# Exp units on GpSimd outside the span of branch B, a scaling step moved to GpSimd, and corrected operation times in a planned kernel

## Chip, cores, metric

One core of a Trainium2 chip. The metric is device time in microseconds (us) of the whole program. TensorE's clock is granted by a throttle; each run comes with the mean granted share (1.0 is full speed).

## The reference, cut to what matters

Two attention branches over the same input x (2048 tokens, width 512, 32 heads of 16), mixed by a gate:

```python
g = sigmoid((x * gate_w).sum(-1, keepdims=True))
a = A(x)   # full softmax attention: 32 heads x 2048 x 2048 scores
b = B(x)   # each token sees 8 earlier tokens (offsets 0, 2, .. 14)
return g * a + (1 - g) * b
```

Branch A needs 32 x 2048 x 2048 exponentials. The kernel cuts them into 2048 units of 128 keys x 512 queries. Branch B has 16 tiles of 128 tokens; it is mostly elementwise work.

## The kernel before

All instructions are recorded by a planner that runs while the kernel is built. Jobs (Python generators) yield requests such as `("dve", priority, duration, function)`. The planner keeps a clock for each engine, picks the next job from the durations written in the source, and so fixes the instruction order on every engine. A duration in the source is therefore no work, but it decides the order.

The exps of branch A take two ways. ScalarE takes three units or two in one instruction (buffers `ring` -> `pT`):

```python
def act_tail(k, parts, rname, rslot, ring, n):
    ...
    def f():
        st["pT"] = work.tile([128, 3 if k % 2 == 0 else 2, QW], BF16, name="pT", tag=pname, bufs=2)
        A.activation(out=st["pT"][:, 0:n, :], in_=ring[:, 0:n, :], func=ACT.Exp,
                     scale=LN2 / 128.0, bias=-VOFF * LN2 / 128.0)
    yield ("act", k, 0.050 + 0.4267 * n, f)
    ...
```

VectorE takes single units ("riders" that TensorE adds to a ring step when a `w` bank of PSUM is free), as a cubic polynomial on the bits, in four operations that read PSUM:

```python
def dve_unit(p, t, j, s, ds, wt, n):
    lo = wt[:].bitcast(U16).rearrange("p (n two) -> p n two", two=2)[:, :, 0]
    ...
    yield ("dve", pr, VP, e1)                  # ta = lo * A3
    yield ("dve", pr, VP, lambda: e23(A2))     # ta = (ta + A2) * lo
    yield ("dve", pr, VP, lambda: e23(A1))     # ta = (ta + A1) * lo
    yield ("dve", pr, VP, e4)                  # pd = ta + const + scores, as 16-bit integers
```

Branch B runs on GpSimd, but its softmax has one wide step on VectorE, which the plan takes for 0.34 us:

```python
def b_attn(t, rel, prio):
    ...
    def attn():
        V.scalar_tensor_tensor(out=lg[:], in0=lg[:], scalar=omg[:, t:t + 1], in1=bc(st["ss"]), op0=ALU.mult,
                               op1=ALU.mult)
    yield ("dve", prio, 0.34, attn)
    ...
```

The planner also issues "fillers" into planned gaps of TensorE: matmuls with a zero weight tile (`acc<-ident,z`) that add nothing and are meant to keep the clock up.

## Time and profile before

| | before |
|---|---|
| first three runs | 877.56, 877.6, 881.56 us |
| the profiled run | 881.81 us (span 880.0), granted clock 0.98 |
| exp units: ScalarE / VectorE | 1814 in 726 instructions / 234 |
| first exp starts, last exp ends | 19.1, 868.3 us |

The profiled run is one of the slower ones of this kernel.

The page's span and busy times: engine, busy us, share of the span, instructions.

```profile
span 880.0 us, 15956 instructions
PE 771.3 (88%) x6062; PEld 268.1 (30%) x6062; DVE 767.9 (87%) x1346; ACT 842.6 (96%) x758; POOL 619.4 (70%) x594
```

The page's slices of before: each digit is a fortieth of the span, busy share in tenths; PEclk is the granted clock.

```profile
POOL 2000283899797889898898989897989898965000
PEclk9799999999999999999999999879999999999999
```

ScalarE (ACT) has almost no room. GpSimd (POOL) is idle in the second to fourth slices and in the last three. The clock is below full in a few slices.

The page's chain of waits, by engine and then by engine, tile and line:

```profile
ACT 48%; PE 22%; issue 19%; DVE 11%; DMA 0%; ACTq 0%
ACT pT L288 47%; PE w L288 8%; PE ring L288 7%; PE acc L288 6%; DVE ta L288 5%; DVE pd L288 1%; DVE lg L288 1%; PE heat L288 1%; PE last L288 0%; ACT lg L288 0%; DVE accS L288 0%; DVE ssum L288 0%; PE xt L288 0%; DVE kvs L288 0%; DVE kpk L288 0%
```

Half of the chain is the exps.

Groups of instructions of before with forms kept apart: engine, operation, out<-in, shapes, count, then busy us and the mean ns of one, then idle time before them and what ended it.

```profile
L288 ACT ACTIVATE pT<-ring 128x1536 bf16<-128x1536 f32 x363 | 544.9, 1501 | 13.8 <-PE ring L288 7.4 <-PE w L288 3.2 <-PE acc L288 0.3
L288 ACT ACTIVATE pT<-ring 128x1024 bf16<-128x1024 f32 x362 | 390.5, 1079 | 6.1 <-PE ring L288 3.5 <-PE w L288 1.9
...
L288 DVE SCALAR_TENSOR_TENSOR lg<-lg,omg,ssum 128x256 f32<-128x256 f32 x16 | 14.2, 886 | 0.1
```

The exps overlap their neighbours, so the durations overstate their cost. From start to start the median is 1.33 us for three units and 0.90 us for two, 2.23 us a pair. The scaling took 0.89 us on average; single ones took 0.465 to 1.531 us.

Busy times of before in stretches (PE, PEld, DVE, ACT, POOL, then granted clock, DMA share, GB/s):

```profile
30.00:35.00 5.00, 5.00 (x36) 1.37 (x35) 2.22 (x6) 4.52 (x5) 0.00 (x0) 0.50 0.00 0
...
285.00:290.00 5.00, 4.40 (x25) 1.03 (x25) 3.12 (x5) 3.22 (x4) 4.69 (x6) 0.66 0.15 39
580.00:585.00 5.00, 4.80 (x31) 1.22 (x28) 3.84 (x7) 4.19 (x5) 4.92 (x6) 0.50 0.00 0
```

In these stretches TensorE had half its clock for all or part of the time, and ScalarE was idle for 0.5 to 1.8 of 5 us. In the trace's clock record of this run there are five such stretches before the tail, 3.4, 6.8 or 10.2 us long, and only the values 1.0 and 0.5. That agrees with the Trainium skill's "TensorE: Matmul & The Clock Gate" (Part 1), which has a free-running window of 3413 ns and two clock states.

### The profile page before, as it was taken

To read this page: it belongs to the slowest core of one execution; us is meant where nothing else is said; L and a number is where in the kernel's file an instruction comes from. 1 tells how busy PE (TensorE), PEld (TensorE's weight loads), DVE (VectorE), ACT (ScalarE), POOL (GpSimd) and SP (SyncE) were. 2 spreads that over 40 slices of the span, in tenths; PEclk is the share of its full clock that TensorE was granted. 3 is DMA by queue.
4 is the path that set the end of the run, shared out by engine and by line. 5 is a ranking of instruction groups with operands and counts; after the bars stand their busy time and mean duration, and the time that the engine had idled before them with its cause. 6 is when DMAs were issued, how large, how long until landed. Compare 5 with 4: busy or idle time off the path is not lost.

```text
span 880.0 us, 15956 instructions
## 1 busy us (share of the span) xinstructions
PE 771.3 (88%) x6062; PEld 268.1 (30%) x6062; DVE 767.9 (87%) x1346; ACT 842.6 (96%) x758; POOL 619.4 (70%) x594
## 2 busy tenths in 40 slices
PE   8999889998898888889899998888798988888886
PEld 4232333333223232223333232223232222223222
DVE  4789899988989799989987888988988989989885
ACT  5999999999999999999999999999999999999995
POOL 2000283899797889898898989897989898965000
PEclk9799999999999999999999999879999999999999
DMA  8002203331414230321131312303021230200000
GB/s 288 2 1 96 80 24 120 108 122 29 150 32 144 67 115 19 114 67 42 30 104 31 125 50 95 103 7 109 1 74 60 84 115 7 64 4 7 1 1 25
DMA packets 55710, 59.78 MB, mean 68 GB/s; under 512 B 3649, under 2 KB 52289, under 8 KB 55633
## 3 DMA queue, kind: packets, MB, share of 16 engines
q1 hardware_dynamic: 54816, 58.50, 21.0%
q8 instruction: 47, 0.77, 0.4%
q10 hardware_dynamic: 816, 0.26, 0.1%
q14 instruction: 31, 0.25, 0.1%
HBM read 46.14 MB, written 12.62 MB: 67 GB/s over the span
## 4 chain that ended last, share of the span: by engine, by line
ACT 48%; PE 22%; issue 19%; DVE 11%; DMA 0%; ACTq 0%
ACT pT L288 47%; PE w L288 8%; PE ring L288 7%; PE acc L288 6%; DVE ta L288 5%; DVE pd L288 1%; DVE lg L288 1%; PE heat L288 1%; PE last L288 0%; ACT lg L288 0%; DVE accS L288 0%; DVE ssum L288 0%; PE xt L288 0%; DVE kvs L288 0%; DVE kpk L288 0%
## 5 line engine op out<-in xcount | busy, mean ns | idle before, releaser
L288 ACT ACTIVATE pT<-ring 128x1536 bf16<-128x1536 f32 x726 | 830.1, 1290 | 19.9 <-PE ring L288 10.9
L288 PE MATMUL ring<-qt,kt_all 32*128 32x512 bf16 x1878 | 294.2, 387 | 87.0 <-ACT pT L288 77.0
L288 DVE SCALAR_TENSOR_TENSOR ta<-ta,w 128x512 f32<-128x512 f32 x468 | 308.3, 679 | 5.0
L288 POOL TENSOR_TENSOR prod<-prod 128x512 f32<-128x512 f32 (+1 forms) x208 | 241.7, 1175 | 6.3
L288 PE MATMUL acc<-pT,vp_all 128*17 128x512 bf16 x1814 | 230.8, 390 | 0.1
L288 PEld LDWEIGHTS <-kt_all 32*128 32x128 bf16 x2112 | 104.8, 91 | 334.7 <-issue 320.0
L288 DVE TENSOR_SCALAR ta<-w 128x512 f32<-128x512 uint16 x234 | 157.9, 684 | 39.8 <-PE w L288 38.6
L288 PE MATMUL acc<-ident,z 128*32 128x512 bf16 (+6 forms) x750 | 168.6, 340 | 5.9 <-DVE accS L288 5.4
L288 DVE SCALAR_TENSOR_TENSOR pd<-ta,w 128x512 uint16<-128x512 f32 x234 | 156.4, 678 | 2.6
L288 POOL TENSOR_TENSOR prod<-ksh,qb 128x512 f32<-128x512 bf16 x128 | 145.7, 1164 | 11.4 <-DVE ta L288 9.3
L288 POOL TENSOR_TENSOR prod<-vsh,lg 128x512 f32<-128x512 bf16 x128 | 136.7, 1100 | 10.5 <-DVE lg L288 8.2
L288 PE MATMUL w<-qt,kt_all 32*128 32x512 bf16 x234 | 88.0, 389 | 1.0 <-DVE osb L288 0.6
L288 POOL TENSOR_SCALAR mq<-qpk 128x512 f32<-128x512 bf16 x12 | 7.4, 615 | 108.0 <-DVE qpk L288 108.0
L288 PE MATMUL acc<-pd,vp_all 128*17 128x512 bf16 x234 | 81.1, 390 | 0.2
L288 PEld LDWEIGHTS <-z 128*32 128x32 bf16 x774 | 51.9, 95 | 82.7 <-issue 65.5
L288 PEld LDWEIGHTS <-vp_all 128*17 128x17 bf16 x2048 | 44.5, 88 | 90.3 <-issue 88.0
L288 PE MATMUL w<-bw,xT 128*128 128x512 bf16 x192 | 51.2, 390 | 3.2 <-DVE pd L288 1.6
L288 PEld LDWEIGHTS <-xT 128*128 128x128 bf16 x512 | 31.7, 98 | 38.1 <-issue 25.1
L288 POOL TENSOR_TENSOR lg<-lg,mx 128x256 f32<-128x256 f32 x16 | 10.1, 630 | 37.4 <-DVE mx L288 37.3
L288 DVE CAST kvs<-w 128x512 bf16<-128x512 f32 x32 | 21.9, 686 | 12.5 <-PE w L288 12.5
L288 DVE COPY accS<-acc 128x512 f32<-128x512 f32 (+1 forms) x32 | 21.5, 673 | 1.8 <-ACT accS L288 1.5
L288 POOL TENSOR_TENSOR obb<-ob,prod 128x512 bf16<-128x512 f32 x16 | 20.4, 1272 | 1.3
(110 smaller groups left out, 437.4 us busy)
## 6 DMA issues: line engine op xcount, KB each, us to landing
ksh<-kv_scr SPq DMA_DIRECT2D x16, 1024.0 KB
vsh<-kv_scr SPq DMA_DIRECT2D x16, 1024.0 KB
kv_scr<-kvs SPq DMA_DIRECT2D x16, 256.0 KB
kt_all<-k_scr SPq DMA_DIRECT2D x6, 512.0 KB
q_scr<-qpk SPq DMA_DIRECT2D x24, 128.0 KB
qt<-q_scr SPq DMA_DIRECT2D x24, 128.0 KB
xr<-in_A_x_dram SPq DMA_DIRECT2D x4, 512.0 KB
out_dram<-osb SPq DMA_DIRECT2D x14, 128.0 KB
```

What stands on the lines that cost most here:

```text
L288: return chain_on(self._key, f(*a, **k))
```

## The change

The intent: GpSimd is idle before branch B starts and after it ends, so let it compute exp units there. VectorE copies the scores from PSUM to SBUF (a buffer that branch B uses for its values, lent outside its span), and GpSimd evaluates the cubic in six operations. Branch B's scaling moves from VectorE to GpSimd as two operations. GpSimd's durations in the plan are set to what traces show, and what GpSimd delivers is used 2.5 us later than planned (slack). A rule adds a filler to a ring step when the plan sees TensorE busy under 40% of the last 3.4 us.

```diff
-    LAT = {"pe": 0.17, "act": 0.22, "dve": 0.12, "pool": 0.12, "sp": 0.08}
+    LAT = {"pe": 0.17, "act": 0.22, "dve": 0.12, "pool": 0.02, "sp": 0.08}
...
+                if (shut is not None and any(row_left[shut])
+                        and P.have(P.now + dur) < THIN * P.HAM):
+                    more += fill_pass(0.2134, P.now) + 0.01
...
+    def pool_unit(p, t, j, s, hs, wt, n):
+        sc, y, z = psc[0][:, hs, :], psc[0][:, 2, :], psc[0][:, 3, :]
+        ...
+        yield ("dve", 39, VP, lambda: V.tensor_copy(out=sc, in_=wt[:]))
+        yield ("rel", "w", s)
+        ...
+        yield ("pool", 0, 0.70, lambda: G.tensor_scalar(out=y, in0=lo, scalar1=YA, scalar2=YA * YS, op0=ALU.mult,
+                                                        op1=ALU.add))
+        yield ("pool", 0, 1.34, lambda: G.tensor_tensor(out=z, in0=y, in1=y, op=ALU.mult))
+        yield ("pool", 0, 0.70, lambda: G.tensor_scalar(out=z, in0=z, scalar1=1.0, scalar2=YB, ...))
+        yield ("pool", 0, 1.34, lambda: G.tensor_tensor(out=z, in0=z, in1=y, op=ALU.mult))
+        yield ("pool", 0, 1.34, lambda: G.tensor_tensor(out=z, in0=z, in1=sc, op=ALU.add))
+        ...                                        # fin: pd = z + const, as 16-bit integers, 0.70
+        yield ("delay", SLACK)
...
-                yield ("pool", gp, 1.11, mul_k(hf, w_))
-            yield ("pool", gp, 1.22, add_k(8, 0, 2))
+                yield ("pool", gp, 1.12, mul_k(hf, w_))
+            yield ("pool", gp, 1.30, add_k(8, 0, 2))
... (the other durations of GpSimd likewise)
-        def attn():
-            V.scalar_tensor_tensor(out=lg[:], in0=lg[:], scalar=omg[:, t:t + 1], in1=bc(st["ss"]), ...)
-        yield ("dve", prio, 0.34, attn)
+        yield ("pool", -4, 0.40, lambda: G.tensor_scalar(out=st["ss"][:], in0=st["ss"][:], scalar1=omg[:, t:t + 1], ...))
+        yield ("pool", -4, 0.72, lambda: G.tensor_tensor(out=lg[:], in0=lg[:], in1=bc(st["ss"]), op=ALU.mult))
...
         yield ("rel", "ob", 0)
+        yield ("delay", SLACK)
```

## The prediction

> **What bounds it now.** ScalarE. The page's busy table has it busy 842.6 of 880.0 us; the chain of waits runs through its exps (pT) for 47% of the span. They start at 19.12 us and end at 868.3 us, with 11.7 us of tail: 726 instructions, 1814 of the 2048 units of 128x512; VectorE does 234. In an undisturbed stretch of the timeline (834.76 on, 30 instructions in 33.58 us) one averages 1.12 us, a unit 0.45 us. 726 x 1.12 = 813 us; the other 36 us are branch B's 16 small exps (0.47 us each), about 14 us of visible waits, and late starts that the pipeline partly hides. The windows tie the worst waits to TensorE's granted clock: 0.50 to 0.66 around 25-37, 285 and 580-590 us. In the waits view nobody waits notably for GpSimd; it waits 37 us for VectorE's row maximum. It is idle before 88 us (but for setup) and after 804 us.
>
> **What changes.** Counted in the built programs' instruction order, 22 units go to GpSimd, 12 before branch B and 10 after. But VectorE's fall from 234 to 224, so ScalarE loses only 12 units, five instructions (726 to 721).
> - A GpSimd unit, from like operations: three two-input (1.28 us each) and three one-input (0.62 to 0.72): about 5.9 us. The Trainium skill's GPSIMD Engine Reference (Specifications) gives GpSimd no PSUM access, hence a VectorE copy, 0.68 us; a VectorE unit costs 4 x 0.68 = 2.7 us. 22 units fill 130 us of idle GpSimd.
> - Branch B's attention scaling leaves VectorE (16 x 0.89 us) for two GpSimd operations (estimate 0.4 + 0.65 us). The same section says that GpSimd contends with VectorE operations with two SBUF inputs; the trace agrees: this one took 0.465 to 1.531 us.
> - VectorE: -27 us of exps, +15 of copies, -14 of scaling: about 742 busy. GpSimd: +147, about 766.
> - GpSimd's corrected times only reorder. GpSimd was never late for anyone, so they remove no wait directly. The slack protects TensorE's in-order queue. Filler matmuls are added where TensorE has been thinly busy, but filler columns barely change (204k to 199k).
>
> **On the critical path.** Five exp instructions at 1.12 us, less 0.5 us for the odd single-unit one that goes: about 5 us. I add 2 us for waits, from a looser VectorE and better placed filler. Start and tail are unchanged; VectorE's relief is off the path.
>
> **Prediction.** 877.6 - 7 = 870.5 us, range 864 to 877. Faster by over 2% (under 860): 0.08; within 2%: 0.90; slower: 0.02.
>
> **What the profile would show.** Right: 721 pT instructions, the last ending near 861 to 862 us, pT busy about 824 us; the three-plus-two pair still 2.24 us; GpSimd working from near 25 to near 855 us; tail 11 to 12 us; no wait for a GpSimd result over 1 us. Wrong on waits: clock dips (windows under 0.7) gone or new, 1 to 3 us of exp time each. Wrong on unit cost: GpSimd operations over 1.4 us, with TensorE or VectorE waiting for them.
>
> **What would make it wrong.** Clock dips falling elsewhere: before's three runs already spread 4 us (877.56 to 881.56). If those at 25-37 and 580-590 us vanish, it ends near 864. If GpSimd in branch B, with about 1 us more per tile and nearly full (36 to 38 of each 40 us), falls behind, the in-order VectorE waits for its logits and all slips, to 877 or more.

## The result, and the profile after

| | before | after |
|---|---|---|
| first rounds, median (range) | 878.73 (877.56 to 881.56), 4 runs | 867.38 (865.5 to 869.42), 4 runs |
| ratio | | 0.9867, 95% interval 0.9832 to 0.9901 |
| later rounds | 879.91 (876.83 to 882.41), 11 runs | 870.11 (868.11 to 872.68), 6 runs |
| ratio | | 0.9891, 95% interval 0.9869 to 0.9914 |

A ratio is the mean time of one kernel's runs over that of the other's of the same rounds, so it is not quite the ratio of the medians. The gain is 1.1 to 1.3%, 10 to 11 us; both medians lie in the predicted range of 864 to 877 us.

The page's span and busy times of after:

```profile
span 865.4 us, 16034 instructions
PE 755.1 (87%) x5977; PEld 268.1 (31%) x6038; DVE 751.1 (87%) x1312; ACT 836.0 (97%) x753; POOL 750.4 (87%) x758
```

The slices of after, for GpSimd and the clock:

```profile
POOL 2586995999898989999999999998999999978883
PEclk9999999999999999999999999989999999999999
```

The chain of waits of after:

```profile
ACT 52%; issue 20%; PE 19%; DVE 9%; POOL 0%; another core or an unknown queue 0%; ACTq 0%; DVEq 0%
ACT pT L292 51%; PE w L292 6%; PE ring L292 6%; PE acc L292 5%; DVE ta L292 4%; DVE pd L292 1%; ACT lg L292 1%; DVE kpk L292 1%; PE heat L292 1%; DVE kmax_pk L292 1%; PE last L292 1%; PE xt L292 0%; DVE crow L292 0%; ACT xT L292 0%; DVE accS L292 0%
```

GpSimd's idle ends are filled, the clock dips are fewer, and the "DVE lg" entry has left the chain. Still, ScalarE's exps are the chain, now for 51% of the span.

Groups of after, forms kept apart:

```profile
L292 ACT ACTIVATE pT<-ring 128x1536 bf16<-128x1536 f32 x360 | 547.6, 1521 | 12.0 <-PE ring L292 8.2 <-PE acc L292 0.6 <-PE w L292 0.5
L292 ACT ACTIVATE pT<-ring 128x1024 bf16<-128x1024 f32 x361 | 396.5, 1099 | 1.0 <-PE ring L292 0.4 <-PE acc L292 0.2
...
L292 POOL TENSOR_TENSOR psc<-psc 128x512 f32<-128x512 f32 x66 | 78.8, 1193 | 5.2
L292 POOL TENSOR_SCALAR psc<-psc 128x512 f32<-128x512 f32 x22 | 13.6, 620 | 1.9
L292 POOL TENSOR_SCALAR psc<-psc 128x512 f32<-128x512 uint16 x22 | 13.6, 618 | 32.4 <-DVE psc L292 31.5
L292 POOL TENSOR_SCALAR pd<-psc 128x512 uint16<-128x512 f32 x22 | 13.6, 617 | 1.9
L292 POOL TENSOR_TENSOR lg<-lg,ssum 128x256 f32<-128x256 f32 x16 | 10.1, 631 | 0.2
...
L292 POOL TENSOR_SCALAR ssum<-ssum,omg 128x32 f32<-128x32 f32 x16 | 5.8, 363 | 7.2 <-DVE ssum L292 7.0
```

A GpSimd unit takes (78.8 + 3 x 13.6) / 22 = 5.4 us. ScalarE does 721 exp instructions. Its idle time before them fell from 13.8 + 6.1 to 12.0 + 1.0 us.

**Where the time went, term by term.** From each trace I took the starts of the exps. "At pace" is the count of three-unit and two-unit instructions times 1.331 and 0.904 us (the medians from start to start), with 0.48 us for the one single-unit instruction of before. "Excess" is the rest between the first exp's start and the last one's end: waits, and branch B's 16 small exps. The part "in dips" is the lateness of instructions that started in a half-clock stretch or up to 3 us after it.

| profiled run | exps | first exp | at pace | excess (in dips + rest) | tail after the last exp | span |
|---|---|---|---|---|---|---|
| before | 726 | 19.1 | 810.9 | 38.3 (9.9 + 28.5) | 11.7 | 880.0 |
| after | 721 | 19.9 | 805.5 | 30.2 (2.4 + 27.8) | 9.9 | 865.4 |
| difference | -5 | +0.7 | -5.4 | -8.1 (-7.5 - 0.7) | -1.8 | -14.6 |

This pair is 14.6 us apart because before's profiled run was a slow one; the medians are 10 to 11 us apart. So of the gain, 5.4 us are five fewer exps, and about 5 to 6 us are fewer waits and a shorter tail. The experiments ask what made the second part.

Part of the tail shows in ScalarE's waits. In before, the last output copy (osc) waited for VectorE's osb; in after it did not. The first line is of before, the columns are total us, times, longest us:

```profile
ACT osc L288 <- DVE osb L288: 5.9, 1, 5.9
```

And the same wait in after, two in all:

```profile
ACT osc L292 <- PE last L292: 4.6, 2, 4.2
```

### The profile page after: what moved, and what is told of

Read it like the earlier page. It is cut to its first block, busy times and chain, and to the rows that moved or that the text cites. A ratio compares the mean times of both kernels' runs of the same rounds, so it can differ in the third digit from the quotient of the medians. Undisturbed runs are those within 1.5% of the kernel's fastest.

```text
span 865.4 us, 16034 instructions
## 1 busy us (share of the span) xinstructions
PE 755.1 (87%) x5977; PEld 268.1 (31%) x6038; DVE 751.1 (87%) x1312; ACT 836.0 (97%) x753; POOL 750.4 (87%) x758
## 4 chain that ended last, share of the span: by engine, by line
ACT 52%; issue 20%; PE 19%; DVE 9%; POOL 0%; another core or an unknown queue 0%; ACTq 0%; DVEq 0%
ACT pT L292 51%; PE w L292 6%; PE ring L292 6%; PE acc L292 5%; DVE ta L292 4%; DVE pd L292 1%; ACT lg L292 1%; DVE kpk L292 1%; PE heat L292 1%; DVE kmax_pk L292 1%; PE last L292 1%; PE xt L292 0%; DVE crow L292 0%; ACT xT L292 0%; DVE accS L292 0%
## 5 line engine op out<-in xcount | busy, mean ns | idle before, releaser
L292 ACT ACTIVATE pT<-ring 128x1536 bf16<-128x1536 f32 (+1 forms) x721 | 823.5, 1310 | 13.0 <-PE ring L292 8.7
L292 PE MATMUL ring<-qt,kt_all 32*128 32x512 bf16 x1874 | 290.1, 383 | 92.1 <-ACT pT L292 78.8
L292 DVE SCALAR_TENSOR_TENSOR ta<-ta,w 128x512 f32<-128x512 f32 x448 | 297.7, 681 | 5.9
L292 PE MATMUL acc<-pT,vp_all 128*17 128x512 bf16 x1802 | 225.0, 385 | 0.1
L292 DVE TENSOR_SCALAR ta<-w 128x512 f32<-128x512 uint16 x224 | 151.6, 685 | 38.0 <-PE w L292 37.1
L292 PE MATMUL acc<-ident,z 128*32 128x512 bf16 (+4 forms) x717 | 162.0, 339 | 2.0 <-DVE accS L292 1.8
L292 DVE SCALAR_TENSOR_TENSOR pd<-ta,w 128x512 uint16<-128x512 f32 x224 | 150.8, 680 | 2.7
L292 POOL TENSOR_TENSOR psc<-psc 128x512 f32<-128x512 f32 x66 | 78.8, 1193 | 5.2
L292 POOL TENSOR_SCALAR psc<-psc 128x512 f32<-128x512 uint16 (+1 forms) x44 | 27.2, 619 | 34.4 <-DVE psc L292 31.5
L292 PE MATMUL w<-bw,xT 128*128 128x512 bf16 x161 | 47.5, 381 | 3.3 <-issue 0.5
```

The lines of the kernel that those rows point to most:

```text
L292: return chain_on(self._key, f(*a, **k))
```

## The experiments

Twelve kernels ran, all correct. The first four take parts of the change in or out of the source, so the planner makes a new order each time. The next ones (5 to 10) keep the order of one kernel exactly and alter only what is issued; the traces agree. Two more are re-plans of the whole change.

My theory at the start (A): the gain is a sum, 5 us from fewer exps and the rest mostly from the filler rule that keeps the clock up. Rivals: all of it hangs on the GpSimd units (B), or none of it does (C).

### 1. The change without GpSimd's exp units

```diff
-    P.spawn(psc_job(ev_lent), 16.0)
-        if t == NT - 1:
-            yield ("spawn", psc_job(None))
```

> The kernel after with GpSimd's exp units taken out and all else kept (new operation times, slack, scaling on GpSimd, filler rule): by the built program 725 exp instructions, 236 VectorE units, none on GpSimd. Theory A (the gain is a sum: about 5 us from five fewer exp instructions, the other 6 us from fewer waits, mostly the filler rule against clock dips): about 872 to 873 us, ratio to before near 0.993, granted clock near 0.99. Rival B (all of the gain hangs on the GpSimd units): about 877 us, ratio 0.999. Rival C (the units give nothing, the rest all): about 867 us.

Measured: 884.89 us (876.7 to 888.03), ratio to before 1.0029 (0.9981 to 1.0078). Two runs took 876.7 us at a clock of 0.986, four 884.7 to 888.0 us at 0.966 to 0.973. By the median all three numbers that I had written were missed; the two faster runs lie at rival B's 877. The profiled run had ten half-clock stretches before the tail and 22.2 us of exp excess in dips. So the new order had a trouble that neither before nor after has.

### 2. GpSimd's exp units alone, on the kernel before

The edit: from after, the old operation times and latency, `THIN = 0.0`, the scaling back on VectorE at 0.34, no slack for branch B's result.

> The complement: GpSimd's exp units (with their own slack) on the kernel before; old operation times, no slack for branch B's result, scaling on VectorE, no filler rule. 720 exp instructions (1799 units), 228 VectorE units, 21 on GpSimd. Theory A: six fewer exp instructions, about 6.5 us, and the clock dips of before remain: about 872 us, ratio 0.993, clock near 0.98. Rival B: 867 us. Rival C: 878 us.

Measured: 893.48 us (886.97 to 897.62), ratio 1.0152 (1.0111 to 1.0193): slower than before, with six fewer exps. The profiled run has a clock of 0.994 and 45.2 us of excess outside dips. One wait of ScalarE alone, at 112 us, where GpSimd goes over to branch B, took 6.05 us. A low clock is not needed to lose time.

### 3. The change without the filler rule

```diff
-    THIN = 0.40
+    THIN = 0.0
```

> The kernel after without the filler rule of the ring step (which adds 4 fillers in all, three of them between 25 and 31 us of the plan). 720 exp instructions. Theory A: the dip of the clock at 25 to 40 us is back, about 2 us of exp time, and others may be: about 870 to 872 us, clock 0.98. Rival D (the rule does nothing, waits fell because VectorE is freer): about 867 us, and the dip at 25 to 40 us costs nothing.

Measured: 883.32 us (880.73 to 887.26), ratio 1.0033 (0.9998 to 1.0067), clock 0.967 to 0.979. Theory A expected 870 to 872 us; against after's later median of 870.1 this lost some 13 us. Either four fillers are worth that, or the new order is to blame; experiment 6 tells.

### 4. The filler rule alone, on the kernel before

The edit: the lines of the rule, with `THIN = 0.40`, added to before.

> The kernel before with only the filler rule added (3 fillers in all). 725 exp instructions, 237 VectorE units. Theory A: 1 us for one exp instruction and about 2 us or more for the dip at the start: 873 to 876 us, clock 0.985 to 0.99. Rival D: 877 us.

Measured: 888.41 us (881.66 to 893.47), ratio 1.0085 (1.004 to 1.0129), clock 0.965 to 0.984. The stretch at half clock near 25 us was gone in the profile, but five others came elsewhere. Theory A's number fails.

The four together: each part, alone or left out, gives a kernel as slow as before or slower. As costs these differences cannot be added up. Taking a part out also draws a new order, and that alone moves the time by as much as the effect that is looked for.

### 5. After once more, beside the next three

> The kernel after, unchanged, beside the next three on one chip. From the runs so far a kernel's time moves by 0.3 to 0.4 us for each us that TensorE spends at half clock; before, taken to zero half-clock time at 0.4, is at about 869.5 us and after at 862.4. Expected: 866 to 869 us, clock 0.990 to 0.995, ratio 0.986 to 0.988. If after was only lucky in its first runs: 870 us or more at a clock near 0.985.

Measured: 870.11 us (868.11 to 872.68), ratio 0.9891 (0.9869 to 0.9914), clock 0.981 to 0.993. The gain holds in later rounds, a little smaller. But the time and most of the clocks missed what was expected (866 to 869 us at 0.990 to 0.995): the median clock was 0.987, which is what I had written for a first draw that was partly lucky.

### 6. The order of after, without its four fillers

```diff
+                    mute[0] = True       # matmuls of the filler are not issued; the plan's time stays
                     more += fill_pass(0.2134, P.now) + 0.01
+                    mute[0] = False
```

> The instruction order of after is kept exactly, but the four fillers of the new rule are not issued. Theory E (the filler itself keeps the clock up at 25 to 36 us; the 883 us of the kernel without the rule came from the new order that it brought): the dip at the start is back, about 10 us of half clock, so 869 to 872 us, clock 0.985 to 0.988. Rival F (the fillers are worth the 16 us that the kernel without the rule lost): about 880 us. Rival G (they do nothing): same as after.

Measured: 870.0 us (868.94 to 870.49), ratio 0.9885 (0.9862 to 0.9908): the same as after beside it. The dip at the start did come back. The exps in the first 40 us of this run (busy us, count, granted clock, DMA share, GB/s):

```profile
0.00:40.00 40.00, 18.86 (x17) 0.87 0.50 159
```

and of after's first profiled run:

```profile
0.00:40.00 40.00, 20.14 (x18) 1.00 0.49 159
```

One exp less by 40 us, but not in the total time. So the four fillers are worth nothing that these rounds resolve, and the 13 us of experiment 3 came from the order that the missing rule led the planner to. F is refuted and G holds (theory E's 869 to 872 us was met as well, but only because after itself came at 870.1 us); of theory A the filler's share falls.

### 7 and 8. More fillers in an unchanged order

```diff
+                lo = P.now + dur - P.HAM
+                seen = sum(min(b, P.now + dur) - max(a, lo) for a, b in P.streamed if b > lo)
+                if (shut is not None and any(row_left[shut])
+                        and seen + extra_fill(P.now + dur) < 0.50 * P.HAM):
+                    fill_pass(0.2134, P.now)      # issued, but no time for it in the plan
+                    extra.append(P.now)
```

> The order of before is kept exactly; 39 fillers of 512 columns are added into ring steps where the plan sees TensorE busy under half of the last 3.4 us. Theory E (clock dips cost before about 10 us of its exp time and nothing else need change): the half-clock time falls from about 26 us to 10 or less, and the time to 870 to 874 us. Rival H (dips are a symptom, not a cause: TensorE is thin because ScalarE waits anyway): clock rises but the time stays at 878 to 881 us, or rises by the fillers' own 8 us of TensorE.

Measured on before: 879.96 us (877.31 to 882.61), ratio 0.9998 (0.9975 to 1.0021), clock 0.985 to 0.997. The half-clock time (2 x (1 - clock) x span) fell from a median of about 28 us for before's runs to 15 us, and the time did not move; the 870 to 874 us of theory E are missed.

> The same addition (37 more fillers) on the order of after. Theory E: half-clock time from about 12 us to near 3 (the tail), time 863 to 865 us, a version better than both. Difference to the filled kernel before: about 7 us, the part of the change that is not clock (5 us of exp instructions and about 2 of waits and tail). Rival H: 867 us or more.

Measured on after: 868.49 us (866.65 to 869.94), ratio 0.987 (0.9845 to 0.9894), clock 0.993 to 1.0. That is 1.6 us under after beside it (0.9891), with intervals that overlap: not shown to be better. Theory E's 863 to 865 us are missed.

What follows: among the runs of one kernel, time and half-clock time do go together, at 0.2 to 0.4 us for each us at half clock (0.31 over the 29 runs of before beside the experiments). By that slope the 13 us of half-clock time bought back on before should give about 4 us. They gave nothing. Rival H, that the dips are a symptom, would explain that. So would dips that do cost 4 us, bought back with 39 fillers that cost TensorE about as much (39 x 0.2134 us = 8.3 us in the plan's terms). The runs do not separate the two; shown is only that buying the clock back this way does not pay.

### 9. The order of after, its 22 GpSimd units as exps on ScalarE

```diff
-        yield ("pool", 0, 0.70, lambda: G.tensor_scalar(out=y, ...))      # and four more
+        for d in (0.70, 1.34, 0.70, 1.34, 1.34):
+            yield ("pool", 0, d, lambda: None)
...
-            G.tensor_scalar(out=st["pd"][:].bitcast(U16), in0=z, ...)
+            A.activation(out=st["pd"][:], in_=sc, func=ACT.Exp, scale=LN2 / 128.0, bias=-VOFF * LN2 / 128.0)
```

> The order of after is kept exactly on TensorE and VectorE; the 22 units that GpSimd computed (132 operations, about 120 us of GpSimd) are instead 22 single exp instructions on ScalarE, each after VectorE's copy as before. If ScalarE is the bound, each is paid in full: 22 x about 0.48 us = 10.6 us, so about 880 us, as slow as before. If GpSimd's units cost something in waits, less than that. If ScalarE is not the bound there: 870 us.

Measured: 881.92 us (878.43 to 884.79), ratio 1.0019 (0.9972 to 1.0066). Against after's ratio of 0.9891 that is 1.3%, some 11 us, for an expected 10.6. GpSimd lost 120 us of work and nothing became faster. The intervals leave about 5 us either way, but the profiled runs agree: the excess is 41.9 us with the 22 single exps in it, 10.6 us above experiment 5's 31.3. So ScalarE pays for the units in full, and GpSimd's units cost nothing visible. In after, then, the 22 units are worth 11 us to ScalarE; but VectorE gave up 10 of its own (234 to 224), so the change as a whole keeps 12 units, 5.4 us.

### 10. The order of after, the scaling back on VectorE

```diff
-        yield ("pool", -4, 0.40, lambda: G.tensor_scalar(out=st["ss"][:], ...))
-        yield ("pool", -4, 0.72, lambda: G.tensor_tensor(out=lg[:], ...))
+        yield ("pool", -4, 0.40, lambda: None)
+        yield ("pool", -4, 0.72, lambda: V.scalar_tensor_tensor(out=lg[:], in0=lg[:], scalar=omg[:, t:t + 1],
+                                                                in1=bc(st["ss"]), op0=ALU.mult, op1=ALU.mult))
```

> The order of after with branch B's attention scaling back on VectorE (16 operations of 0.47 to 1.5 us at the places in the order where GpSimd had them). VectorE is busy 14 us more. If VectorE's relief is off the path (my prediction): 869 to 872 us, as after_again. If the relief is what cut the waits: 875 us or more, with more of ScalarE's exp waits at full clock.

Measured: 878.78 us (877.97 to 884.97), ratio 1.0007 (0.9949 to 1.0064), clock 0.970 to 0.982. Sixteen operations, 13.7 us of VectorE in all, take back about 9 us of the 10 (10 us by the ratios, with some 6 us either way; the intervals do not overlap). My prediction had this relief off the path; it is not. The excess of the profiled run is 41.9 us (12.3 in dips), against 31.3 (4.2) for experiment 5. So of the 10.6 us added, 8.1 lie in and just after half-clock stretches; whether these cost the time or only go with it is open here too.

ScalarE's exps wait longer for TensorE (total us, times, longest us). This run:

```profile
ACT pT L292 <- PE ring L292: 14.2, 24, 2.9
ACT pT L292 <- PE w L292: 5.0, 6, 2.3
```

and after:

```profile
ACT pT L292 <- PE ring L292: 8.7, 14, 2.9
ACT pT L292 <- PE w L292: 0.5, 1, 0.5
```

Experiment 5 has 8.4 and 2.0 us there, before 10.9 and 5.1.

Since the order is the same, one place can be laid beside itself. First this run, VectorE and then TensorE, in order of time (start, us, what, idle before and releaser):

```profile
321.23 1.12 DVE L292 SCALAR_TENSOR_TENSOR lg<-lg,omg,ssum 128x256 f32<-128x256 f32 x1
322.28 0.68 DVE L292 TENSOR_SCALAR ta<-w 128x512 f32<-128x512 uint16 x1
322.99 1.41 DVE L292 SCALAR_TENSOR_TENSOR ta<-ta,w 128x512 f32<-128x512 f32 x2
324.32 0.68 DVE L292 TENSOR_SCALAR qb<-w 128x512 bf16<-128x512 f32 x1
...
325.05 1.02 PE L292 MATMUL w<-bw,xT 128*128 128x512 bf16 x4 [0.94 <-DVE qb L292]
326.01 0.39 PE L292 MATMUL ring<-qt,kt_all 32*128 32x512 bf16 x3
```

The exps there:

```profile
326.51 5.97 ACT L292 ACTIVATE pT<-ring 128x1536 bf16<-128x1536 f32 x5 [0.77 <-PE w L292]
```

and the clock just after:

```profile
330.00:335.00 5.00, 4.70 (x25) 0.90 (x27) 4.62 (x8) 4.99 (x6) 4.84 (x5) 0.56 0.00 0
```

The same instructions in after:

```profile
319.01 0.69 DVE L292 TENSOR_SCALAR ta<-w 128x512 f32<-128x512 uint16 x1 [0.19 <-PE w L292]
319.74 1.41 DVE L292 SCALAR_TENSOR_TENSOR ta<-ta,w 128x512 f32<-128x512 f32 x2
321.06 0.68 DVE L292 TENSOR_SCALAR qb<-w 128x512 bf16<-128x512 f32 x1
...
321.80 1.02 PE L292 MATMUL w<-bw,xT 128*128 128x512 bf16 x4 [0.18 <-DVE qb L292]
322.76 0.39 PE L292 MATMUL ring<-qt,kt_all 32*128 32x512 bf16 x3
```

The scaling takes 1.12 us. VectorE copies qb out of a `w` bank late; TensorE wants that bank for the next projection (w<-bw), waits 0.94 us instead of 0.18, and the scores for the ring behind it come late; ScalarE is idle 0.77 us; then the clock halves. In after, ScalarE has no such wait at this place:

```profile
315.16 11.80 ACT L292 ACTIVATE pT<-ring 128x1024 bf16<-128x1024 f32 x10
```

Why the scaling is at times so long on VectorE can be read from the traces as well. Five traced runs have it there (before and experiments 2, 4, 7 and 10), 80 operations in all. For 65 of them GpSimd was in, or within 0.04 us of starting, an operation with two inputs that had over 0.19 us to go. Every one of these 65 ended 0.278 to 0.287 us after that GpSimd operation ended. The other 15 took 0.465 to 0.476 us. So its length follows what GpSimd happens to be doing, which the plan does not know.

Before has the same chain in its own order. Its chain of waits in order of time, start and us:

```profile
280.07 1.29 DVE lg L288
281.37 3.58 DVE ta L288 x6
284.95 0.61 DVE pd L288
285.56 0.04 issue
285.60 1.87 PE w L288 x4
287.47 0.54 PE ring L288 x2
```

A scaling of 1.38 us (planned 0.34) stands first in these lines (other VectorE work precedes it), and the exp at its end starts 1.51 us late, in the stretch of 285 to 290 us at clock 0.66 that is printed above. That could have been read before the change was ever run.

How far this goes: the plan of after has no time on VectorE for these operations, while before's plan had 0.34 us for each. Unplanned VectorE time is thus 13.7 us here and 14.2 - 16 x 0.34 = 8.8 us in before. So the 9 us are what the operation costs in after's order, not exactly what before paid for it. No run takes the scaling off VectorE in before's order.

### 11 and 12. Two re-plans of the whole change

> Nothing of the change is taken away: the slack constant is 2.4 instead of 2.5, which makes the plan choose another order (721 exp instructions, 1803 units, 21 on GpSimd). If the change's parts make the gain: 867 to 872 us, clock 0.985 or more. If a good part of the gain, and the losses of the four re-planned part kernels, come from which order the plan happens to give: 875 to 890 us, clock 0.97 to 0.98.

Slack 2.4 instead of 2.5: 870.75 us (870.51 to 871.94), ratio 0.9897 (0.986 to 0.9933). The same gain. But this is hardly another draw: in the traces VectorE's sequence is the same as in after up to 680 us, GpSimd's to 684 and ScalarE's to 724 us. It does not show that after's order was not a lucky one.

> Another re-plan of the whole change: GpSimd may take units down to 12 left in a period instead of 20. 719 exp instructions (1797 units), so 2.2 us less for ScalarE than after, and an odd number, which in the six orders seen so far went with the short tail (9.5 to 9.9 us against 11.2 to 12.3). By the sum: 866 to 868 us. By the lottery of the order: 875 to 890 us.

Units allowed down to 12 left in a period (`PMIN = 12`): 881.47 us (877.53 to 882.8), ratio 1.0008 (0.9964 to 1.0053), with two exp instructions fewer than after. The 866 to 868 us of the sum are missed; it lies where I had put the lottery of the order (875 to 890). This order differs from after's from 40 us on, so of the two orders of the whole change that really differ one keeps the gain and one loses it. ScalarE again has one wait of 6.42 us, at 114.6 us, as experiment 2 had at 112. The tail was 11.1 us although the number of exps is odd, so the rule of odd numbers that I had read out of six orders is wrong.

## Why the prediction was right, and where it was not

- **The bound.** ScalarE's exps; right. After, they are 51% of the chain, and experiment 9 shows units put back on ScalarE paid in full.
- **Five fewer exp instructions, about 5 us.** Right: 721, 5.4 us at pace; pT busy 823.5 us (predicted 824); the pair still 2.23 us.
- **Costs of operations.** A GpSimd unit 5.4 us (predicted 5.9), GpSimd 131 us busier (predicted 147), VectorE 17 us less busy (predicted 26). All too large the same way. Of a unit's three two-input operations, the square y * y took 1.04 us and only the other two 1.26 to 1.28, and the one-input ones took 0.62. VectorE's operations issued back to back overlap in the trace (841 us summed, 768 busy, in before), so there count times mean duration overstates the busy time. The count of filler columns in the prediction (204k to 199k) came from a listing that was cut; the whole programs have 307.6k and 294.9k. The conclusion, little change, stands.
- **Waits, 2 us.** This is the term that was mis-sized. It measured about 5 to 6 us at the medians with the tail in it; the profiled pair shows 8.1 us less excess and 1.8 us less tail. That is why the last exp ended at 855.6 us and not at 861 to 862, and why the time came out at 867.4 and 870.1 instead of below by only 7. That 870.1 lies so near the predicted 870.5 us is in part luck: the prediction started from 877.6 us, and before's median in those rounds was 879.9.
- **"VectorE's relief is off the path."** Wrong, and the likeliest reason for the size. In after's unchanged order 13.7 us of scaling put back on VectorE cost about 9 us. VectorE's idle share does not tell; at the places looked at, a late operation held a PSUM bank that TensorE waited for. The scaling was planned at 0.34 us and measured at 0.89. It is not the whole story: experiments 1 and 3 have the scaling on GpSimd too, and in their orders the exps still waited 8.5 and 8.4 us for TensorE's `w` matmuls.
- **"Better placed filler."** Nothing: experiment 6. Experiment 3 seemed to say the opposite by 13 us, through its new order.
- **Start and tail unchanged.** The start is (19.9 for 19.1 us), the tail is not (9.9 for 11.7 us). Only the place of the last output copies was seen to differ; the cause was not tested.
- **No wait for a GpSimd result over 1 us.** Right: the longest in after is 0.4 us.
- **"Clock dips falling elsewhere".** They did, and they go with the time from run to run; but fillers that halved them on before gained nothing.
- **The order.** The prediction let the corrected times "only reorder" and had no term for the order that is drawn. That a good order was drawn is luck, as far as the prediction goes: with the order of experiment 12 the same change takes 881.5 us, outside the range.

What stays open. Why some orders (experiments 1 to 4 and 12) lose 11 to 23 us against after: part is dips, part the 6 us hole near 112 us in two of them. The chain of waits into that hole runs through VectorE (5.6 us of `ta` and `pd` in a row in experiment 2, 7.3 us of VectorE in experiment 12) and not through GpSimd; why the plan came to that was not traced. What the corrected times and the slack give by themselves: they exist only through the order, so no run with a kept order can tell. And whether a right duration for the scaling on VectorE would have served as well as moving it.

## What to carry to other kernels

Where one engine is the bound, count what leaves it: 22 units were moved but 12 counted, since another helper gave up 10. An engine with idle time can still be on the path, if a late operation of it holds a buffer that the engine feeding the bound is waiting for; look in the chain of waits for small entries whose duration differs from what the schedule assumes. And in a kernel whose schedule is computed, a part taken out of the source draws a new schedule: keep the order and alter only what is issued, or the schedule's luck (here 13 us, experiment 3 against 6) is taken for the part's cost.

## What the Trainium skill lacked or had wrong

- "GPSIMD Engine Reference" (Specifications) says that GpSimd contends with VectorE operations with two SBUF inputs, but that row gives no duration. Here one such operation of 128x256 f32 took 0.465 to 0.476 us undisturbed; with a two-input GpSimd operation under way it ended 0.278 to 0.287 us after that one, so it took up to 1.56 us (mean of all 0.86 to 1.09). On GpSimd the plain multiplication of that shape took 0.621 to 0.637 us in all 16 cases.
- The same page (Performance versus the Vector engine) gives 769 ns as measured for a best case of 512 elements on GpSimd. The one-input operations of 128x512 here took 617 to 620 ns on average, less than this best case; the same passage also has 1.03 cycles per element for bodies of up to two operations, an estimate of 512 x 1.03 / 1.2 GHz = 0.44 us, so the measured time lies between the page's two figures. Its figure of about 2.6 cycles per element for two inputs would be an estimate of 512 x 2.6 / 1.2 GHz = 1.11 us; the new operations took 1.19 us on average (1.04 where both inputs are the same tile, 1.26 to 1.28 otherwise), so that one fits roughly.
- "TensorE: Matmul & The Clock Gate" (Terms) puts the penalty of throttled time at time x (1 - K/N), 0.5 us for each us at half clock. In this kernel, bound by ScalarE, the whole time moved by 0.2 to 0.4 us between runs of one kernel, and halving the half-clock time with fillers gained nothing.
- No page follows one late VectorE operation step by step, from the PSUM bank that it holds up to the wait of the engine that bounds the kernel. One such case is in experiment 10 (1.12 us of VectorE, 0.94 us of TensorE waiting, 0.77 us of ScalarE; then clock 0.56 in the stretch from 330 us).
